# First chunk of an mLSTM and act-GCU kernel: the weight conversions in another order of steps, w_out's second piece ahead of the turning, the clamp on GpSimd

## The chip, the cores and the metric

The kernel runs on 1 core of a Trainium2 chip. The metric is the device time of one execution in microseconds (us). Before the change the median of 3 runs is 540.6 us (539.52 to 541.74).

## The reference, cut to what matters

```python
# B, H, S, D = 4, 8, 768, 40; n_tokens, d_model, d_ff = 3072, 320, 2048
def _attn_ref(q, k, v, i_gate, f_gate, o_gate):       # mLSTM cell, one step per t
    m_new = maximum(f[t] + m, i[t])
    C = exp(f[t] + m - m_new) * C + exp(i[t] - m_new) * outer(v[t], k[t])
    n = exp(f[t] + m - m_new) * n + exp(i[t] - m_new) * k[t]
    y[t] = sigmoid(o[t]) * (C @ q[t]) / maximum(abs(n . q[t]), 1.0)
    ...
def _moe_ref(x, w_in, w_out):                         # x: y as (3072, 320)
    h = x @ w_in                                      # 320 x 2048
    g = h * np.cos(h)
    return (g @ w_out).astype(np.float32)             # 2048 x 320

out["moe_" + k] = m[k]                                # float64
```

`w_in` and `w_out` (`np.random.randn` times a scale) reach the chip as float64, as pairs of 32-bit words. The kernel makes float32 of them itself. That conversion is what the change is about.

## The kernel before, in words

The sequence of 768 is cut into 6 chunks of 128 (`NC = 6`). One cell `n = c * B + b` is the mLSTM of chunk `c` and batch entry `b`, 8 heads at a time. `first_cells` does the cells of chunk 0. Then `both_parts(c, b)` runs for every chunk and every `b` of 0 to 3. It does cell `n = (c + 1) * B + b` of the next chunk beside a quarter of the second part for chunk `c`: `g = h * cos(h)` for 512 columns of `w_in`. It has two halves, `i = 0` and `i = 1`, each for 256 columns, `f2 = 2 * b + i`. I call `both_parts(0, b)` step b.

The order of the instructions on each engine is the order of the code (`tc.manual_schedule()`). Engines meet through semaphores, and a waiting instruction holds all behind it on its engine.

In a half, TensorE makes `h` for the 256 columns in two PSUM tiles `pup` (lines 639 and 645; two tiles in all, so the next half begins when the gates of this one are done). ScalarE rounds it (`near`, L653), VectorE takes the rest (`rest`, L656), ScalarE takes the sine (L661), VectorE multiplies (`gate`, L665). TensorE's product with `w_out` for the half before (`down`, L677) fills in between. Half 0 also has the cell's scores (L479), the weighting by them (`weigh`, L485), the values (L505 to L514), the normalising (L523 to L534, whose last product makes `xT`) and GpSimd's `fade` (L580). Half 1 has the cell's state (L622) and prepares the next cell: `turn_blocks` turns q and k with two VectorE transposes (L452), GpSimd scales q (`scale_q`, L461) and k (`weigh_k`, L407), and in step 1 ScalarE also copies low dimensions (L444).

The conversion. A piece is 128 rows by 512 elements of `w_in` (two for each step, p0 and p1), 128 by 256 of its last rows (`w_in_l`, the low piece), or 128 by 640 of `w_out`. It goes through five operations:

- ScalarE, `take_apart`: the absolute value of the high word taken as a float (L150), then the low word scaled (L152)
- VectorE, `put_together`: the clamp (L157), the two shifts in one instruction (L159), the sign put in with an `or` (L161, which reads the raw words too)
- GpSimd, `put_together`: the add of the low word's part (L162)

Raw words land in buffers that rotate: `pb`, 4 buffers, for `w_in`, and `pc`, 3 buffers, for `w_out`. The load of a piece into a buffer waits until the add (L162) of the piece that had it before is done. `w_out` has 8 pieces, o0 to o7: `next_out` converts the next one and issues the load of the piece 3 later. All these loads are issued by SyncE's queue (SP), one after the other, L180 for `w_out`, L139 (p0, then p1, four DMAs each) and L174 (low, four DMAs) for `w_in`.

Step b uses `w_in`'s pieces that were converted in the step before: step b's code converts p0, p1 and low for step b + 1, loads those for step b + 2 (`weights_in(b + 2)`, L1046), and converts `w_out` pieces o(2b) in half 0 and o(2b+1) in half 1. Where each conversion stands before the change:

- half 0, after the gates: p0 (L993, in steps 1 and 2), then `w_out` (L995)
- half 0, after the normalising: p0 in step 0, p1 in steps 1 and 2 (L1039)
- half 1, between `rest` and the state: p1 in step 0, low in steps 1 and 2 (L1002)
- half 1, after the gates: low in step 0 (L1013)
- half 1, at the end, after `weights_in` and after `turn_blocks` and `scale_q`: `w_out` (L1053)

In `first_cells` three pieces are converted, two of them with ScalarE's part done early.

Of the kernel before, what the change touches and what calls it, by code (L numbers as in the profile page):

```python
# [11 lines left out]
FP = mybir.dt.float32  # L12
I32 = mybir.dt.int32
# [3 lines left out]
OP = mybir.AluOpType  # L17
# [12 lines left out]
def kernel(  # L30
# [20 lines left out]
    nc = tc.nc  # L51
# [87 lines left out]
            nc.sync.dma_start(out=bits[rows, 0:n], in_=piece)  # L139
        return bits  # L140

    def to_float32(dst, bits):
        take_apart(dst, bits)
        put_together(dst, bits)

    def take_apart(dst, bits):
        n = dst.shape[1]
# [3 lines left out]

        nc.scalar.activation(out=bits[:, 0:n, 0], in_=lo, func=AF.Copy, scale=2.0 ** -29)  # L152

    def put_together(dst, bits):
        n = dst.shape[1]
        hi, t, m = bits[:, 0:n, 1], dst.bitcast(I32), bits[:, 0:n, 0]
        nc.vector.tensor_scalar(out=t.bitcast(FP), in0=t.bitcast(FP), scalar1=LEAST, scalar2=GREATEST,  # L157
                                op0=OP.max, op1=OP.min)
        nc.vector.tensor_scalar(out=t, in0=t, scalar1=5, scalar2=2, op0=OP.logical_shift_left,  # L159
                                op1=OP.logical_shift_right)  # L160
        nc.vector.scalar_tensor_tensor(out=t, in0=hi, scalar=TOP2, in1=t, op0=OP.bitwise_and, op1=OP.bitwise_or)  # L161
        nc.gpsimd.tensor_tensor(out=t, in0=t, in1=m, op=OP.add)  # L162

# [665 lines left out]
    def first_cells():  # L829
        nc.vector.memset(nil, 0.0)  # L830
        gates_in()
        nc.scalar.copy(out=ident_b, in_=ident)
        load(0, "qk")
        later_gates_in()
        load(0, "v")
        load(1, "qk")
        load_o(0, (0, 1))
        load(1, "v")
        load(2, "qk")
        load_E(0)  # L840
        load_E(1)
        warm(12)
        wall_in(0, 0, pmu)
        wall_in(0, 1, psum_o())
        gates_first()
        gates_first_out()
        spread(0, 0)
        decay_exponents_half(0, 0)
        turn(0)
        turn_out(0, False)  # L850
        gates_sums()
        spread(0, 1)
        decay_exponents_half(0, 1)
        decay(0)
        weigh_k(0)
        load_E(2)
        load(2, "v")
        load_E(3)
        load_o(0, (2, 3))
        load(3)  # L860
        pieces.extend(weights_in(0))
        wall_in(1, 0, psum_o())
        wall_in(1, 1, psum_o())
        gates_less_sums()
        spread(1, 0)
        decay_exponents_half(1, 0)
        scores(0)
        gates_maxima()
        turn(1)
        weigh(0)  # L870
        sigmoid(0, slice(0, 2))
        turn_out(1, False)
        spread(1, 1)
        decay_exponents_half(1, 1)
        gates_exponents()
        decay(1)
        weigh_k(1)
        values(0)
        normalize(0)
        scores(1)  # L880
        gates_exp()
        turn(2)
        turn_out(2, False)
        warm(2)
        seam(0)
        weigh(1)
        seam_out(0)
        state(0)
        load_two(B, "qk")
        decay_exponents(2)  # L890
        gates_diagonal()
        decay(2)
        weigh_k(2)
        values(1)
        load_E(B)
        normalize(1)
        scores(2)
        turn(3)
        sigmoid(0, slice(2, 4))
        seam(1)  # L900
        load_two(B, "Kv")
        load_E(B + 1)
        load_o(1)
        outs.append((0, weights_out(0)))
        weigh(2)
        decay_exponents(3)
        turn_out(3)
        seam_out(1)
        values(2)
        decay(3)  # L910
        weigh_k(3)
        state(1)
        normalize(2)
        scores(3)
        pg = gates_turn()
        warm(1)
        seam(2)
        weigh(3)
        to_float32(*pieces.pop(0))
        decay_exponents(B)  # L920
        pieces.extend(weights_in(1))
        outs.extend((p, weights_out(p)) for p in range(1, 3))
        seam_out(2)
        state(2)
        for piece in pieces[0:2]:
            take_apart(*piece)
        gates_keep(*pg)
        values(3)
        normalize(3)
        put_together(*pieces.pop(0))  # L930
        warm(3)
        seam(3)
        seam_out(3)
        put_together(*pieces.pop(0))
        low_dimensions(B)
        turn_blocks(B)
        state(3)
        load_E(B + 2)
        decay(B)
        sigmoid(1)  # L940
        weigh_k(B)
        odd_values(B)
        scale_q(B)
# [5 lines left out]

        nc.scalar.activation(out=spot, in_=spot, func=AF.Sin)  # L950

    def next_out():
        p, piece = outs.pop(0)
        to_float32(*piece)
        if p + 3 < NF // 2:
            outs.append((p + 3, weights_out(p + 3)))

    def both_parts(c, b):

        n = (c + 1) * B + b  # L960
        cell = n < N
        for i in range(2):
            f2 = 2 * b + i
            up = Up(c, f2)
            if cell and i == 0:
                scores(n)
                if c == 0 and b == 0:

                    warm(8, psum_o())
            if cell and i == 1:  # L970
                if n % 2 == 1 and n > B + 1 and n + 3 < N:
                    load_two(n + 3, "Kv")
            for e in range(2):
                up.near(e)
            for e in range(2):
                up.rest(e)
            if i == 0:
                if cell:
                    weigh(n)
                    if n + 1 < N:  # L980
                        decay_exponents(n + 1)
                    if n == B:
                        clear_low()
                for e in range(2):
                    up.sin(e)
                    up.gate(e)
                if c > 0:
                    sums(c, f2)
                if b == 0 and c == 1:
                    sigmoid(c + 1)  # L990

                if c == 0 and b > 0 and pieces:
                    to_float32(*pieces.pop(0))  # L993
                if c == 0:
                    next_out()  # L995
                if cell and n + 1 < N:
                    decay(n + 1)
            else:
                if cell:
                    seam_out(n)  # L1000
                if pieces:
                    to_float32(*pieces.pop(0))  # L1002
                if cell:
                    state(n)
                for e in range(2):
                    up.sin(e)
                    up.gate(e)
                if c > 0:
                    sums(c, f2)
                if n == B + 1:  # L1010
                    low_dimensions(n + 1)
                while pieces:
                    to_float32(*pieces.pop(0))  # L1013
                if cell and n + 1 < N:
                    weigh_k(n + 1)
                    odd_values(n + 1)
            if i == 1 and b == B - 1 and 0 < c < NC - 2:
                sigmoid(c + 2)
                sin_next()
            down_slot(c, f2)  # L1020
            if f2 == 0 and c > 1:
                for p in range(2):
                    combine_first(c - 1, p)
            if cell and i == 0:
                turn_gate(n)
                values(n)
                seam(n)
                normalize_turned(n)
                fade(n)
                if c == 1 and b < 3:  # L1030
                    weight_sums(b + 1)
                if n % 2 == 1 and n > B + 1 and n + 3 < N:
                    load_two(n + 3, "qk")
                if n > B + 1 and n + 3 < N:
                    load_E(n + 3)
                if b == B - 2 and c + 2 < NC:
                    load_o(c + 2)
                if c == 0 and pieces:
                    to_float32(*pieces.pop(0))  # L1039
                sin_next()  # L1040
            if f2 == 0 and c > 1:
                for p in range(2):
                    combine(c - 1, p)
            if i == 1:
                if c == 0 and b + 2 < B:
                    pieces.extend(weights_in(b + 2))  # L1046
                    load_two((n + 3) // 2 * 2)
                    load_E(n + 3)
                if cell and n + 1 < N:
                    turn_blocks(n + 1)  # L1050
                    scale_q(n + 1)
                if c == 0:
                    next_out()  # L1053
                if (c, f2) == (0, LAST):
                    weight_sums(0)

    pieces, outs = [], []
# [41 lines left out]
```

## Time and profile before

| | us |
|---|---|
| median of 3 runs | 540.6 (539.52 to 541.74) |
| the profiled execution | 540.66 |
| its span | 538.9 |
| TensorE (PE) busy in the span | 520.1 |
| VectorE (DVE) | 421.9 |
| ScalarE (ACT) | 285.7 |
| GpSimd (POOL) | 224.7 |
| mean granted TensorE clock | 0.972 |

The busy times are of the whole span. The change touches about 37 to 146 us of it, so the tables by stretch and the timeline of that stretch say more than the sums. In the timeline each row has its start, its length, its engine and line, what it writes and reads, and in brackets the idle time ahead of it and what ended it.

### The profile page before, as it was taken

What the parts mean: (1) busy time and instruction counts of PE and PEld (TensorE: products, weight loads), DVE (VectorE), ACT (ScalarE), POOL (GpSimd) and SP (SyncE); (2) the same over time, 40 slices, a digit from 0 to 9 for tenths busy, and PEclk for the clock granted to TensorE, in tenths of its full rate; (3) what the DMA queues carried; (4) which work ended last, traced back from release to release, by engine and by line L of the source; (5) the groups of instructions that cost most, each with busy time, mean ns of one, the idle gap of its engine ahead of it and who ended that gap; (6) DMA issues with size and microseconds to landing.
All of it is one profiled execution on the core that took longest, in us unless ns stands there. A gap on an engine that the chain in (4) does not pass through costs nothing.

```text
span 538.9 us, 10497 instructions
## 1 busy us (share of the span) xinstructions
PE 520.1 (97%) x3844; PEld 353.7 (66%) x3844; DVE 421.9 (78%) x907; ACT 285.7 (53%) x546; POOL 224.7 (42%) x369
## 2 busy tenths in 40 slices
PE   7999879899999999999999999999999999999996
PEld 4885445545566767757767767767667767576755
DVE  5565889998788897898878898878898878663636
ACT  2587958666475446826527826526836522222221
POOL 7435454555477573533542632542421421221211
PEclk9587989999999999999999999999999999999999
DMA  9999884959847539329248329249220000000001
GB/s 137 220 213 233 248 169 142 213 92 253 176 116 171 67 94 191 42 93 202 28 120 174 43 88 193 35 125 174 40 79 7 2 5 6 19 33 1 0 1 49
DMA packets 99939, 57.81 MB, mean 107 GB/s; under 512 B 62304, under 2 KB 92608, under 8 KB 99888
## 3 DMA queue, kind: packets, MB, share of 16 engines
q1 hardware_dynamic: 96496, 55.64, 47.4%
q10 hardware_dynamic: 3248, 1.33, 1.2%
q8 instruction: 30, 0.49, 0.4%
q0 software_dynamic: 144, 0.18, 0.1%
q14 instruction: 21, 0.17, 0.1%
HBM read 51.71 MB, written 4.11 MB: 104 GB/s over the span
## 4 chain that ended last, share of the span: by engine, by line
PE 73%; DMA 9%; DVE 8%; SPq 4%; POOL 2%; ACT 1%; issue 1%; DVEq 0%; POOLq 0%
PE pup L645 26%; PE acc L755 24%; PE pup L639 8%; PE po L677 3%; PE late L755 3%; DMA bits<-in_moe_w_in_dram 3%; PE ps L479 3%; PE vt L514 2%; PE vt L505 2%; PE pu L597 1%; DMA E<-M_d 1%; DVE t L452 1%; DMA xL<-xT 1%; DMA bits<-in_moe_w_out_dram 1%; DMA G<-G_d 1%
## 5 line engine op out<-in xcount | busy, mean ns | idle before, releaser
L645 PE MATMUL pup<-xT,w_in_sb 128*128 128x512 f32 x384 | 177.8, 606 | 4.8 <-DVE g L665 4.5
L653 ACT ACTIVATE n<-pup 128x512 int32<-128x512 f32 x96 | 54.0, 595 | 195.3 <-PE pup L639 143.7
L645 PEld LDWEIGHTS pup<-xT,w_in_sb 128*128 128x128 f32 x384 | 70.6, 193 | 92.2 <-issue 87.9
L656 DVE SCALAR_TENSOR_TENSOR n<-pup,n 128x512 f32<-128x512 f32 x96 | 63.1, 687 | 76.3 <-ACT n L653 75.0
L719 POOL TENSOR_TENSOR D<-g 128x128 f32<-128x128 f32 x40 | 19.8, 495 | 218.6 <-DVE g L665 218.6
L661 ACT ACTIVATE n<-n 128x512 f32<-128x512 f32 x96 | 57.6, 627 | 21.8 <-DVE n L656 13.1
L665 DVE SCALAR_TENSOR_TENSOR g<-pup,n 128x512 f32<-128x512 f32 x96 | 61.7, 684 | 4.1 <-ACT n L661 3.5
L755 PE MATMUL acc<-w_out_sb,g 128*128 128x160 f32 x320 | 58.6, 304 | 0.0
L755 PE MATMUL acc<-T,g 128*128 128x160 f32 x320 | 58.0, 301 | 0.1
L639 PE MATMUL pup<-xL,w_in_l 64*128 64x512 f32 x192 | 54.2, 641 | 0.0
L755 PEld LDWEIGHTS acc<-w_out_sb,g 128*128 128x128 f32 x320 | 47.8, 190 | 5.6 <-issue 4.2
L755 PEld LDWEIGHTS acc<-T,g 128*128 128x128 f32 x320 | 48.1, 190 | 3.6 <-issue 2.9
L402 ACT ACTIVATE E<-E,tab 128x128 f32<-128x128 f32 x160 | 49.0, 388 | 0.3
L677 PE MATMUL po<-w_out_sb,g 128*128 128x320 f32 x128 | 36.2, 436 | 1.8 <-POOL w_out_sb L162 1.8
L755 PE MATMUL acc<-T,S 128*128 128x160 f32 x160 | 35.0, 301 | 0.0
L479 PEld LDWEIGHTS ps<-t,t 40*128 40x128 f32 x384 | 26.0, 196 | 11.3 <-issue 6.6
L677 PEld LDWEIGHTS po<-w_out_sb,g 128*128 128x128 f32 x128 | 24.1, 190 | 13.2 <-POOL w_out_sb L162 2.4
L485 DVE TENSOR_TENSOR E<-ps,E 128x512 f32<-128x512 f32 x48 | 30.7, 681 | 0.5 <-PE ps L479 0.5
L461 POOL TENSOR_TENSOR qG<-t,G 128x512 f32<-128x512 f32 x20 | 25.6, 1281 | 13.0 <-DVE t L452 6.5
L639 PEld LDWEIGHTS pup<-xL,w_in_l 64*128 64x128 f32 x192 | 14.5, 185 | 23.3 <-issue 19.0
L755 PE MATMUL acc<-w_out_sb,S 128*128 128x160 f32 x160 | 28.8, 299 | 0.0
L950 ACT ACT_TABLE_LOAD x22 | 28.2, 1283 | 0.4
(175 smaller groups left out, 883.5 us busy)
## 6 DMA issues: line engine op xcount, KB each, us to landing
E<-M_d SPq DMA_DIRECT2D x22, 512.0 KB
qr<-in_q_dram SPq DMA_DIRECT2D x36, 160.0 KB
kr<-in_k_dram SPq DMA_DIRECT2D x36, 160.0 KB
G<-G_d SPq DMA_DIRECT2D x20, 256.0 KB
bits<-in_moe_w_out_dram SPq DMA_DIRECT2D x8, 640.0 KB
bits<-in_moe_w_in_dram SPq DMA_DIRECT2D x32, 128.0 KB
out_dram<-o_sb SPq DMA_DIRECT2D x24, 160.0 KB
ks<-in_k_dram SPq DMA_DIRECT2D x10, 320.0 KB
```

Source lines behind the costliest of these rows:

```text
L402: nc.scalar.activation(out=Es[n][:, h], in_=Es[n][:, h], func=AF.Exp, scale=-1.0, bias=tab[:, c, 0, g:g + 1])
L479: nc.tensor.matmul(ps[j][:, p], kT[r, p], qT[r, p], start=True, stop=True)
L485: nc.vector.tensor_tensor(out=w, in0=pss[n][j], in1=w, op=OP.mult)
L639: nc.tensor.matmul(pu, w_in_l[r, f2], xL[c][r].rearrange("p b t -> p (b t)"), start=ahead, stop=not ahead)
L645: nc.tensor.matmul(pu.rearrange("p (b t) -> p b t", b=B), w_in_sb[:, i, ts(2 * f2 + e, 128)], xT[c][:, i:NK * B:NK], start=(i == 0 and not ...
L653: nc.scalar.activation(out=self.n[e], in_=self.pu[e], func=AF.Copy, bias=0.25)
L656: nc.vector.scalar_tensor_tensor(out=self.n[e].bitcast(FP), in0=self.pu[e], scalar=0.25, in1=self.n[e], op0=OP.add, op1=OP.subtract)
L661: nc.scalar.activation(out=r, in_=r, func=AF.Sin, scale=TWO_PI_DOWN)
L665: nc.vector.scalar_tensor_tensor(out=g, in0=self.pu[e], scalar=TWO_PI, in1=self.n[e].bitcast(FP), op0=OP.mult, op1=OP.mult)
L677: nc.tensor.matmul(po[c][b], gs[c, f][:, ts(b, C)], w_out_sb[:, f], start=(f == 0), stop=(f == NF - 1))
L755: nc.tensor.matmul(a, lhs, rhs, start=start, stop=stop)
L950: nc.scalar.activation(out=spot, in_=spot, func=AF.Sin)
```

## The change

The conversion becomes four loops over any number of pieces: first ScalarE's part of all, then the clamp of all on GpSimd, then the shifts of all, then `or` and add of all. Two pieces of `first_cells` keep the clamp on VectorE. In half 0 of steps 1 and 2 p0 and `w_out` go through it together. In half 1 the conversion between `rest` and the state goes away: all pieces that are left and `w_out` go through together after the gates, ahead of `weights_in`, `turn_blocks` and `scale_q`. In chunk 0 `weigh_k` moves behind `scale_q`.

```diff
-    def to_float32(dst, bits):
-        take_apart(dst, bits)
-        put_together(dst, bits)
+    def to_float32(*made):
+        for dst, bits in made:
+            take_apart(dst, bits)
+        for dst, bits in made:
+            bound(nc.gpsimd, dst)
+        for dst, bits in made:
+            shift_out(dst)
+        for dst, bits in made:
+            put_together(dst, bits)
...
+    def bound(engine, dst):
+        engine.tensor_scalar(out=dst, in0=dst, scalar1=LEAST, scalar2=GREATEST, op0=OP.max, op1=OP.min)
+
+    def shift_out(dst):
+        t = dst.bitcast(I32)
+        nc.vector.tensor_scalar(out=t, in0=t, scalar1=5, scalar2=2, op0=OP.logical_shift_left,
+                                op1=OP.logical_shift_right)
+
     def put_together(dst, bits):
         n = dst.shape[1]
         hi, t, m = bits[:, 0:n, 1], dst.bitcast(I32), bits[:, 0:n, 0]
-        nc.vector.tensor_scalar(out=t.bitcast(FP), in0=t.bitcast(FP), scalar1=LEAST, scalar2=GREATEST,
-                                op0=OP.max, op1=OP.min)
-        nc.vector.tensor_scalar(out=t, in0=t, scalar1=5, scalar2=2, op0=OP.logical_shift_left,
-                                op1=OP.logical_shift_right)
         nc.vector.scalar_tensor_tensor(out=t, in0=hi, scalar=TOP2, in1=t, op0=OP.bitwise_and, op1=OP.bitwise_or)
         nc.gpsimd.tensor_tensor(out=t, in0=t, in1=m, op=OP.add)
...
+        bound(nc.vector, pieces[0][0])
+        shift_out(pieces[0][0])
         put_together(*pieces.pop(0))
...
-    def next_out():
+    def next_out(*made):
         p, piece = outs.pop(0)
-        to_float32(*piece)
+        to_float32(*made, piece)
         if p + 3 < NF // 2:
             outs.append((p + 3, weights_out(p + 3)))
...
-                if c == 0 and b > 0 and pieces:
-                    to_float32(*pieces.pop(0))
                 if c == 0:
-                    next_out()
+                    next_out(*[pieces.pop(0) for _ in range(min(b, len(pieces), 1))])
...
-                if pieces:
-                    to_float32(*pieces.pop(0))
                 if cell:
                     state(n)
...
-                while pieces:
-                    to_float32(*pieces.pop(0))
+                if c == 0:
+                    next_out(*pieces)
+                    pieces.clear()
                 if cell and n + 1 < N:
-                    weigh_k(n + 1)
+                    if c > 0:
+                        weigh_k(n + 1)
                     odd_values(n + 1)
...
                 if cell and n + 1 < N:
                     turn_blocks(n + 1)
                     scale_q(n + 1)
-                if c == 0:
-                    next_out()
+                    if c == 0:
+                        weigh_k(n + 1)
```

On the engines this is 18 clamps fewer on VectorE and 18 more on GpSimd (7 of 512 elements, 3 of 256, 8 of 640). On SP the load of o4 stands ahead of `weights_in(2)` and that of o6 ahead of `weights_in(3)`, where they stood behind them and behind the loads of q, k, v and E that follow.

More of the change, by code (lines that the diff above doesn't have):

```diff
@@ L918, in first_cells @@
         weigh(3)
-        to_float32(*pieces.pop(0))
+        to_float32(pieces.pop(0))
         decay_exponents(B)
@@ L933, in first_cells @@
         seam_out(3)
+        bound(nc.vector, pieces[0][0])
+        shift_out(pieces[0][0])
         put_together(*pieces.pop(0))
@@ L1011, in both_parts @@
                     low_dimensions(n + 1)
-                while pieces:
-                    to_float32(*pieces.pop(0))
+                if c == 0:
+                    next_out(*pieces)
+                    pieces.clear()
                 if cell and n + 1 < N:
-                    weigh_k(n + 1)
+                    if c > 0:
+                        weigh_k(n + 1)
                     odd_values(n + 1)
@@ L1038, in both_parts @@
                 if c == 0 and pieces:
-                    to_float32(*pieces.pop(0))
+                    to_float32(pieces.pop(0))
                 sin_next()
```

## The prediction, before the run

> **What bounds the kernel now.** I read the windows first, cut at the four steps of chunk 0 (busy us of PE, PEld, DVE, ACT, POOL; granted clock, DMA share, GB/s):
>
> ```profile
> 57.40:80.30 22.90, 20.03 (x129) 10.91 (x120) 21.00 (x45) 16.19 (x32) 11.29 (x12) 0.93 0.81 201
> 80.30:103.30 23.00, 21.11 (x145) 12.29 (x144) 21.59 (x45) 17.41 (x35) 11.43 (x13) 1.00 0.69 178
> 103.30:126.30 23.00, 21.38 (x146) 12.48 (x145) 21.57 (x45) 15.08 (x29) 11.19 (x12) 1.00 0.72 149
> 126.30:148.00 21.70, 21.70 (x148) 12.97 (x148) 16.89 (x36) 13.21 (x24) 9.81 (x12) 1.00 0.88 199
> ```
>
> VectorE works 21.0 to 21.6 of 23 us in steps 0 to 2. In step 3, without w_in, TensorE never stops and a step takes 21.7. So 124.68, where step 3's first `down` starts, is the last place where conversions decide. Next TensorE's rows in the timeline, where its idle time stands:
>
> ```profile
> 70.71 5.37 PE L645 MATMUL pup<-xT,w_in_sb 128*128 128x512 f32 x8 [2.41 <-DVE g L665]
> 95.40 3.67 PE L645 MATMUL pup<-xT,w_in_sb 128*128 128x512 f32 x8 [1.19 <-DVE g L665]
> 118.37 3.67 PE L645 MATMUL pup<-xT,w_in_sb 128*128 128x512 f32 x8 [0.94 <-DVE g L665]
> 124.68 4.58 PE L677 MATMUL po<-w_out_sb,g 128*128 128x320 f32 x16 [0.68 <-POOL w_out_sb L162]
> ```
>
> At each step's end it waits for the gate of half 1. The same eight matmuls take 5.37 us after the long wait, since the clock is at 0.50 from 72.5 to 75.5. The idle time of steps 0 to 2 is 6.4 us (2.9, 1.9 and 1.6: stretch less PE busy), 1.7 more are that clock (5.37 for 3.67): 8 us is the most that can be won. Then SP's queue, and VectorE beside GpSimd:
>
> ```profile
> 62.28 0.38 SPq L180 DMA_DIRECT2D bits<-in_moe_w_out_dram  x1
> 62.71 8.50 SPq L139 DMA_DIRECT2D bits<-in_moe_w_in_dram  x8
> ```
> ```profile
> 192.06 0.86 POOL L701 TENSOR_TENSOR T<-w_out_sb 128x320 f32<-128x320 f32 x1
> 193.00 0.86 POOL L702 TENSOR_TENSOR w_out_sb<-w_out_sb 128x320 f32<-128x320 f32 x1
> ```
> ```profile
> 83.50 1.48 DVE L159 TENSOR_SCALAR w_out_sb<-w_out_sb 128x640 int32<-128x640 int32 x1
> 193.27 1.01 DVE L534 TENSOR_TENSOR xT<-yt,db 128x384 f32<-128x384 f32 x1
> ```
>
> Piece p0 for step 2 is issued at 62.71 and read by ScalarE at 79.72: far ahead. The last two rows are VectorE instructions held by GpSimd: the shift takes 0.49 alone and 1.48 beside the add of p0 (83.20 to 84.63); `xT` takes 0.56 alone and 1.01 beside L702, which ends at 193.86.
>
> **Prices** (start to next start, us, for 512 / 640 / 256 elements): shift 0.46 / 0.53 / 0.33, `or` 0.61 / 0.74 / 0.34, add 1.25 / 1.54 / 0.69; ScalarE's pair 1.14 / 1.49 / 0.69; two rests 1.20, state 0.9, two gates 1.2, two transposes 1.87, `fade` 1.35. The clamp on GpSimd is in no row. Nearest is affine_select, also one input with a compare per element: 1.091 for 1024 and 0.292 for 128 elements, a line that gives 0.63 / 0.75 / 0.41. Low bound, the memsets (0.204 for 128, 1.186 for 1312): 0.52 for 512. High bound, the add: 1.30 / 1.57 / 0.74. I take the first: same shape of work. The GPSIMD Engine Reference of the Trainium skill (3.1, Elementwise) gives about one cycle per element for loops of few operations, an estimate of 0.43 plus dispatch for 512; by it the sum below would be about 1 us smaller, and no run so far shows it.
>
> **What goes.** 18 clamps leave VectorE: 7 x 0.42 + 3 x 0.28 + 8 x 0.49 = 7.7 us, and the three shifts held to 1.44 to 1.48 are freed of 3 x 0.97 = 2.9. GpSimd gets 7 x 0.63 + 3 x 0.41 + 8 x 0.75 = 11.6; it has 11 us of work in 23, so there is room, but the clamps now stand between ScalarE and VectorE, in order. `weigh_k` behind `scale_q` costs nothing: its reader, `pu`, starts over 5 us later. In `first_cells` the clamp (0.63) ends when `weigh` does: nothing.
>
> **What comes, step by step.**
>
> Step 0, half 1. The rests stay at 66.25 (ScalarE's table load sets them). Without p1 ahead of the state the gates end at 69.7, before 71.2: 1.5 won. Now three pieces go together. ScalarE ends the sine at 68.2, then p1 and low; w_out's absolute value ends at 70.8, its clamp at 71.6, so VectorE, its other shifts done, stands until then: shift 72.2, `or` of p1 72.8, low 73.2, w_out 75.25, because add and `or` alternate as L534 and L702 do. Adds: p1 74.5, low 76.0, w_out 77.5. Before, p1 was there at 70.5: step 1's `h` starts its second 128 rows 4 us later, but then has no further gap, and `down` needs the add of 77.5 (before 78.45). About even.
>
> SP. The load of o4 waits for that add, and `weights_in(2)` now stands behind it: 77.5 for 62.7. Two such loads, w_out then p0, take 4.4 us: issued from 62.28, the windows show 112, 275, 234 and 38 GB/s from 62.0 in pieces of 1.5 us, done by 66.7. So p0 lands at L = 81.9; ScalarE wants it at 79.7. Behind p0 in ScalarE's queue stand w_out, the exponentials, p1 and `near`; the twelve loads and those of q and k behind them end before 90, ahead of their readers (93).
>
> Step 1, half 0, from L: p0's value +0.65, clamp +1.36; w_out's value +1.93, clamp +2.78, shift +3.4, both `or` +4.7; the normalising 3.9 more (oT 85.76 to the clamp at 89.68), 0.2 held by `fade`: +8.9. Adds end +7.6, `fade` +8.95, p1's clamp +9.6 (behind `fade`), shift and `or`, +0.2 for the two holding each other: rest at L + 10.9 = 92.8, before 91.21. Half 1: rests, state, gates 3.3: 96.1, before 95.85 (low is no longer in between). Then ScalarE: sine to 94.7, low dimensions 1.7, low 0.7, w_out's value 97.8, clamp 98.6, shift 99.2, `or`s 100.3, transposes 102.2; add of o3 at 102.65. Step 2's rest starts at 102.9, before 100.85.
>
> Step 2, the same with o6 ahead of `weights_in(3)`: L = 102.65 + 4.4 = 107.05 (issued at 92.34 before); rest 118.0 (114.18), gates 121.3 (118.75), ScalarE's w_out value 121.4, clamp 122.2, `or`s 123.9, transposes 125.8, scores 126.8, then step 3's `down`: 126.8, before 124.68. From here TensorE has no gap in either kernel.
>
> Sum: +2.1. Span 538.9 + 2.1 = 541.0; the profiled run is 540.66 and the median 540.6, so 542.7.
>
> SBUF — State Buffer of the Trainium skill (Who interferes with whom) speaks against this change: an instruction of VectorE with two inputs in SBUF and one of GpSimd that reads SBUF exclude each other for their whole length. The trace agrees (1.01 for 0.56). `or` reads two.
>
> **Rivals.**
> - The relief comes through. If the adds come early enough that p0 lands by 79.7 (add of o1 by 75.3), VectorE has 0.42 + 0.49 + 0.97 less behind half 0's gates and 0.42 + 0.55 less before half 1's, TensorE finds the gates done at 93.7 when its `down` ends, and `h`, w_out's shift, `or` and the transposes put step 2's rest at 99.2 (before 100.85); the same again in step 2: -3.3, 537.3. For it: VectorE's own work allows an add at 74.3 to 75.4. Against it: ScalarE's w_out value at 70.8.
> - `or` and add do not hold each other. The three-piece batch ends 1.0 earlier, and three of the four batches behind it, those that lead on to the end, 0.75 each: -3.3 on the sum, 539.4. Against it: L534.
> - Slower: GpSimd's clamp runs at the add's price. In each half 0 w_out's clamp is 0.9 and p1's 0.65 later, in each half 1 w_out's 0.8: 0.8 + 2 x 2.35 = 5.5 more, 548.2. It decides from about 0.75 for 512 elements.
> - The clock. TensorE idles 70.9 to 74.5 in step 0, and up to 1.9 us in steps 1 and 2 (for w_in_l and the gate). Before, 2.4 us of idling were followed by 3.3 us at 0.50, 1.7 us lost. Once or twice more on the path: 544.4 to 546.1. For it: the gap is longer. Against it: step 1's path runs through SP's queue, not TensorE.
>
> **How the numbers follow.** About 0.5% (2.7 us) is what a measurement of this kernel can tell. Forecast 0.38, relief 0.24, no hold 0.14, clamp 0.14, clock 0.10. Predicted 542.7. The forecast's own range is 541 to 544.5 (landing 4 to 5 us after issue, clamp 0.52 to 0.75). The others widen it: 537.0 to 547.5. Faster than 537.9: most of the relief case, 0.22. Slower than 543.3: clamp, clock, and a third of the forecast, 0.38. Within: 0.40.
>
> **What would show it.** SP: L139's second group issued near 77, not 62.7, right after the add of o1; the third near 103. ScalarE idle at L150 in steps 1 and 2, ended by a DMA of w_in. The clamp's mean for 512 near 0.63. Shifts of w_out at 0.49. VectorE busy about 2.5 us less a step, with waits for the clamp in their place. Wrong if ScalarE never waits for w_in, if the clamp is over 1 us, or if step 3's `down` starts before 124.

## The result, and the profile after

| | before | after |
|---|---|---|
| time, median (lowest to highest) | 541.04 us (539.52 to 541.74) | 560.45 us (559.99 to 560.72) |
| ratio, 95% interval | | 1.0368 (1.0339 to 1.0397) |
| profiled run, its span | 540.66, 538.9 us | 559.99, 558.2 us |
| VectorE / GpSimd busy | 421.9 / 224.7 us | 416.2 / 262.2 us |

The change made the kernel 3.7% slower; 0.4% was predicted. The stretches are cut this time where the first `h` of each step starts (columns: stretch; busy us of PE, PEld, VectorE, ScalarE, GpSimd; granted clock, DMA share, GB/s), for the changed kernel:

```profile
43.03:68.43 25.40, 21.00 (x139) 10.85 (x137) 17.25 (x37) 21.87 (x46) 16.64 (x17) 0.92 0.85 230
68.43:103.00 34.57, 24.26 (x145) 13.09 (x145) 21.43 (x41) 16.58 (x33) 24.71 (x19) 0.90 0.59 131
103.00:136.11 33.11, 25.19 (x145) 14.21 (x145) 18.88 (x39) 17.30 (x34) 22.64 (x19) 0.90 0.60 122
136.11:159.15 23.04, 21.43 (x145) 12.48 (x145) 16.97 (x35) 13.76 (x25) 14.86 (x14) 1.00 0.58 149
```

and for the kernel before, with the same cuts:

```profile
46.76:70.71 23.95, 19.51 (x138) 10.52 (x137) 19.01 (x41) 23.67 (x50) 13.03 (x15) 0.97 0.80 228
70.71:95.40 24.69, 23.03 (x145) 12.99 (x145) 22.99 (x47) 16.58 (x33) 12.94 (x14) 0.93 0.72 168
95.40:118.37 22.97, 21.33 (x144) 12.43 (x145) 21.56 (x44) 16.54 (x31) 11.44 (x14) 1.00 0.65 128
118.37:140.22 21.85, 21.17 (x144) 12.60 (x145) 18.09 (x36) 12.78 (x23) 8.58 (x11) 1.00 0.88 221
```

Steps 1 and 2 are 9.9 and 10.1 us longer, steps 0 and 3 1.5 and 1.2. That is 22.7 us (116.12 for 93.46); the span grew by 19.3, because `first_cells` ran 3.7 us faster in this execution. From 15 to 27 us the kernel before had a granted clock of 0.50, the changed one 0.72. The profiles of the experiments start their first `h` at 42.3 to 42.7 or at 46.7 to 46.9 us; kernels in the changed order show both, the three profiles in the old order only the later, and whether the change has a part in it stays open.

In steps 1 and 2 VectorE has less work than before, and GpSimd has twice the work. The groups of GpSimd's clamp in the changed kernel (count; busy us, mean ns of one; idle time before):

```profile
L161 POOL TENSOR_SCALAR w_out_sb<-w_out_sb 128x640 f32<-128x640 f32 x8 | 18.7, 2342 | 8.9 <-ACT w_out_sb L156 5.6 <-DVE g L675 3.2
L161 POOL TENSOR_SCALAR w_in_sb<-w_in_sb 128x512 f32<-128x512 f32 x7 | 13.4, 1918 | 12.1 <-ACT w_in_sb L156 11.8
...
L161 POOL TENSOR_SCALAR w_in_l<-w_in_l 128x256 f32<-128x256 f32 x3 | 3.2, 1061 | 3.5 <-ACT w_in_l L156 3.5
```

One clamp of 512 elements lasts 1.92 us, three times the 0.63 of the prediction and above its upper end of 1.30. Who waits for it stands in the table of waits from 56 to 165 us (total, times, longest):

```profile
DVE w_in_sb L165 <- POOL w_in_sb L161: 15.6, 6, 6.1
...
DVE w_out_sb L165 <- POOL w_out_sb L161: 13.4, 8, 2.4
...
PEld po L687 <- POOL w_out_sb L172: 7.4, 3, 3.9
PE pup L655 <- DVE g L675: 7.2, 3, 3.0
...
PE pup L655 <- POOL w_in_sb L172: 5.6, 1, 5.6
```

VectorE stands 29 us for the clamps of w_in and w_out, and TensorE for what comes behind: the gates, the adds of w_out, and once, at the start of step 1, the add of p1 out of step 0's batch of three pieces. SP's queue, which the prediction followed, and ScalarE's first operation on p0 behind it:

```profile
61.11 18.04 SPq L190 DMA_DIRECT2D bits<-in_moe_w_out_dram  x2
79.20 4.52 SPq L139 DMA_DIRECT2D bits<-in_moe_w_in_dram  x8
...
95.36 16.39 SPq L190 DMA_DIRECT2D bits<-in_moe_w_out_dram  x2
111.80 4.97 SPq L139 DMA_DIRECT2D bits<-in_moe_w_in_dram  x8
```
```profile
85.82 0.67 ACT L156 ACTIVATE w_in_sb<-bits 128x512 f32<-128x512 f32 x1 [1.64 <-DMA bits<-in_moe_w_in_dram]
118.80 0.70 ACT L156 ACTIVATE w_in_sb<-bits 128x512 f32<-128x512 f32 x1 [5.12 <-DMA bits<-in_moe_w_in_dram]
```

w_in for step 2 is issued at 79.20 in place of 62.71, for step 3 at 111.80 in place of 92.34, each time right behind the load of w_out that waits for an add. ScalarE then waits 1.6 and 5.1 us for it. So both suspects are in the trace, one of them larger than thought. TensorE's own lines show what follows:

```profile
103.00 3.67 PE L655 MATMUL pup<-xT,w_in_sb 128*128 128x512 f32 x8 [3.03 <-DVE g L675]
109.88 1.13 PE L649 MATMUL pup<-xL,w_in_l 64*128 64x512 f32 x4 [3.22 <-POOL w_in_l L172]
...
112.75 5.79 PE L687 MATMUL po<-w_out_sb,g 128*128 128x320 f32 x16
...
128.39 6.27 PE L687 MATMUL po<-w_out_sb,g 128*128 128x320 f32 x16 [3.03 <-POOL w_out_sb L172]
136.11 3.67 PE L655 MATMUL pup<-xT,w_in_sb 128*128 128x512 f32 x8 [1.45 <-DVE g L675]
143.60 4.57 PE L687 MATMUL po<-w_out_sb,g 128*128 128x320 f32 x16
```

Behind the longer idle times the same sixteen matmuls take 5.79 and 6.27 us for 4.57: 2.9 us more. The granted clock is 0.79 and 0.73 in these two stretches, 1.00 from 143.60 on. Step 3's first `down` starts at 143.60; it was 124.68.

### The profile page after: what moved, and what is told of

Read it like the earlier page. It is cut to its first block, busy times and chain, and to the rows that moved or that the text cites. A ratio compares the mean times of both kernels' runs of the same rounds, so it can differ in the third digit from the quotient of the medians.

```text
span 558.2 us, 10495 instructions
## 1 busy us (share of the span) xinstructions
PE 522.1 (94%) x3844; PEld 350.7 (63%) x3844; DVE 416.2 (75%) x889; ACT 285.5 (51%) x546; POOL 262.2 (47%) x387
## 3 DMA queue, kind: packets, MB, share of 16 engines
q1 hardware_dynamic: 96496, 55.64, 46.9%
## 4 chain that ended last, share of the span: by engine, by line
PE 73%; DMA 10%; DVE 7%; SPq 3%; POOL 2%; issue 2%; ACT 2%; ACTq 0%; DVEq 0%; POOLq 0%
PE pup L655 25%; PE acc L765 23%; PE pup L649 7%; PE ps L489 4%; DMA G<-G_d 3%; DMA bits<-in_moe_w_in_dram 3%; PE late L765 3%; PE vt L524 2%; PE vt L515 2%; PE po L687 2%; PE pu L607 1%; DMA xL<-xT 1%; SPq L184 1%; PE pw L837 1%; DVE t L462 1%
## 5 line engine op out<-in xcount | busy, mean ns | idle before, releaser
L687 PE MATMUL po<-w_out_sb,g 128*128 128x320 f32 x128 | 39.4, 464 | 4.9 <-POOL w_out_sb L172 4.9
L687 PEld LDWEIGHTS po<-w_out_sb,g 128*128 128x128 f32 x128 | 25.4, 203 | 18.6 <-POOL w_out_sb L172 7.4
L489 PE MATMUL ps<-t,t 40*128 40x128 f32 x384 | 27.8, 286 | 1.3 <-DVE t L462 1.3
```

The source lines that it names most:

```text
L489: nc.tensor.matmul(ps[j][:, p], kT[r, p], qT[r, p], start=True, stop=True)
L687: nc.tensor.matmul(po[c][b], gs[c, f][:, ts(b, C)], w_out_sb[:, f], start=(f == 0), stop=(f == NF - 1))
```

## The experiments

Theory L: the length of GpSimd's clamp, in series between ScalarE and VectorE, costs most. Theory Q: SP's order does, loads of w_in behind a load of w_out that waits for an add. All ratios are to the kernel before.

**1. The clamp back on VectorE** (everything else as changed).

```diff
-            bound(nc.gpsimd, dst)
+            bound(nc.vector, dst)
```


> The changed kernel with its clamps back on VectorE; the order of steps, the groups and SP's order stay as changed. Theory L (length): the clamp's 1.92 us for 512 and 2.34 us for 640 elements on GpSimd, in series between ScalarE and VectorE in each batch, is what costs. Then a batch is shorter by some 1.4 to 1.9 us for each clamp on its path, the add that SP's queue waits for comes 3 to 5 us earlier, and most of the 19.4 us returns: 541 to 546. Theory Q (queue): loads of w_in standing behind the load of w_out on SP are what costs, whatever the clamp's engine. Then only what the clamps themselves last is won, and the third group of w_in loads is still issued near 108 to 111: 551 to 556.

Measured: 544.6 us, 1.012 (1.0069 to 1.0171). About 2.5% of the 3.7 went with the clamp. What is left is more than nothing: ScalarE still waits 2.5 and 4.6 us for w_in.

**2. The load of w_out late.** `next_out` of half 1 converts, and its load is issued at the step's end, behind those of w_in, q, k and E (`late=True` leaves the load out of `next_out`).

```diff
-                    next_out(*pieces)
+                    p = next_out(*pieces, late=True)
...
+                if c == 0 and p < NF // 2:
+                    outs.append((p, weights_out(p)))
                 if (c, f2) == (0, LAST):
```


> The changed kernel with the load of w_out's piece in half 1 issued at the end of the step, behind the loads of w_in, q, k and E; the clamps stay on GpSimd. Theory L: ScalarE no longer waits for w_in, which was 1.6 us in step 1 and 5.1 us in step 2, and nothing else is won, since the clamps stay in series: 553 to 557. Theory Q: the steps are as long as before the change: 541 to 546.

Measured: 553.88 us, 1.0298 (1.0251 to 1.0346): 0.7% won, and no wait of ScalarE for w_in is left. While the clamp is long the queue is the lesser limit.

**3. Both edits.**

> Both edits: clamps on VectorE and the load of w_out behind those of w_in; the changed order of steps and groups is all that is left of the change. Theory L: a little under the run with the clamps on VectorE alone, by the 0 to 3 us that SP's hold still cost there: 538 to 543. Theory Q: about the run with the late load alone, 538 to 544. If the grouping itself costs (VectorE's or-instructions and GpSimd's adds holding each other, 0.8 us a batch): 543 to 546.

Measured: 537.32 us, 0.9976 (0.9943 to 1.0008). Nothing is left of the loss. Against the first run the queue is worth 1.4% here, for 0.7% in the second run. That each of the two hides behind the other would explain it, but the intervals of the four ratios are too wide to show it. The grouping of steps, the rest of the change, costs nothing that can be measured.

**4. The old order with the clamp on GpSimd alone.**

```diff
-        put_together(dst, bits)
+        put_together(dst, bits, nc.gpsimd)
...
-    def put_together(dst, bits):
+    def put_together(dst, bits, engine=nc.vector):
...
-        nc.vector.tensor_scalar(out=t.bitcast(FP), in0=t.bitcast(FP), scalar1=LEAST, scalar2=GREATEST,
+        engine.tensor_scalar(out=t.bitcast(FP), in0=t.bitcast(FP), scalar1=LEAST, scalar2=GREATEST,
```


> The kernel before, with only the clamps of the same 18 pieces moved to GpSimd; order, single pieces and SP's order as before. Theory L: each clamp of 512 elements is 1.9 us in place of 0.42 between ScalarE and VectorE, now piece by piece without another piece's work beside it; the batch before the state in half 1 has two in a row: 555 to 570. Theory Q: SP's order is that of before, so little is lost: 541 to 546.

Measured: 557.83 us, 1.0376 (1.0324 to 1.0429). The clamp alone, in the old order and the old queue, loses as much as the whole change.

**5. The old kernel with the loads of w_in, q, k and E behind the load of w_out.**

```diff
-                if c == 0 and b + 2 < B:
-                    pieces.extend(weights_in(b + 2))
-                    load_two((n + 3) // 2 * 2)
-                    load_E(n + 3)
...
                 if c == 0:
                     next_out()
+                if c == 0 and b + 2 < B:
+                    pieces.extend(weights_in(b + 2))
+                    load_two((n + 3) // 2 * 2)
+                    load_E(n + 3)
```


> The kernel before, with nothing changed but the place of the loads of w_in, q, k and E: at the step's end behind the load of w_out, which waits for an add of GpSimd. Theory Q2 (the queue's hold is a cost of its own, about 7 us, as between the last two runs with the clamp on VectorE): the second group of w_in loads goes out near 78.5 and the third near 103 to 106, 11 us and more later than before, ScalarE waits 2 to 6 us for w_in twice: 544 to 549. Theory S (slack: the hold only hurts together with the grouped order, in which three pieces share a batch): under 1% more, 539 to 542.

Measured: 550.55 us, 1.0184 (1.0146 to 1.0223). Two lines of SP's queue and the table of ScalarE's waits in this kernel:

```profile
79.22 4.59 SPq L139 DMA_DIRECT2D bits<-in_moe_w_in_dram  x8
...
107.28 4.42 SPq L139 DMA_DIRECT2D bits<-in_moe_w_in_dram  x8
```
```profile
ACT w_in_sb L150 <- DMA bits<-in_moe_w_in_dram: 12.8, 2, 7.0
```

The hold is a cost of its own, in the old order too: ScalarE waits 5.8 and 7.0 us, where 2 to 6 us each were expected, and the time lies above the 544 to 549 of theory Q2, so the hold costs more than that theory said.

**6. One operation in place of two** (a look at prices; one run, 561.07 us).

```diff
-            bound(nc.gpsimd, dst)
+            if dst.shape[1] == WP:
+                nc.gpsimd.tensor_scalar(out=dst, in0=dst, scalar1=LEAST, scalar2=None, op0=OP.max)
+            elif dst.shape[1] > WP:
+                nc.gpsimd.tensor_scalar(out=dst, in0=dst, scalar1=1.0, scalar2=None, op0=OP.mult)
+                bound(nc.vector, dst)
+            else:
+                bound(nc.gpsimd, dst)
```


> A look at prices, not at the time: the changed kernel where GpSimd does only the max on pieces of 512 elements (the min is left out), one multiplication by 1.0 on pieces of 640 (their clamp is done by VectorE) and both operations of the clamp on pieces of 256. If each operation of the instruction is a pass over the data: 0.95 to 1.0 us for 512 and 1.2 for 640, 1.06 still for 256. If the form costs 3.7 ns an element whatever it does: 1.92, 2.34 and 1.06.

Measured, in the groups of GpSimd (the third line is affine_select, the row that the prediction took its price from):

```profile
L149 POOL TENSOR_SCALAR w_out_sb<-w_out_sb 128x640 f32<-128x640 f32 x8 | 14.5, 1816 | 12.7 <-ACT w_out_sb L162 12.5
...
L147 POOL TENSOR_SCALAR w_in_sb<-w_in_sb 128x512 f32<-128x512 f32 x7 | 10.5, 1493 | 11.8 <-ACT w_in_sb L162 11.5
L404 POOL TENSOR_SCALAR_AFFINE_SELECT E<-E 128x1024 f32<-128x1024 f32 x7 | 7.7, 1100 | 4.3 <-DMA bits<-in_moe_w_in_dram 3.0 <-DMA E<-M_d 1.2
```

Neither expectation holds. One operation takes 1.49 us for 512 and 1.82 for 640: 2.5 ns an element and 0.2 us, if the max on 512 and the multiplication on 640 cost the same. Two take 3.3 ns and 0.22 us. So the second operation adds 0.8 ns an element; the first, with all else that the instruction does for an element, costs 2.5, near the add of two tensors (1.25 us for 512), and nothing like affine_select (0.9 ns by the prediction's line). Why the two differ so is not settled.

**7. The early p1.** On top of the third run, step 0's half 0 takes one piece of w_in as the other steps do, since the third run's trace showed what still cost: TensorE waits 3.12 us for the add of p1 out of the batch of three, and step 1 takes 26.1 us at a clock of 0.93.

```diff
-                    next_out(*[pieces.pop(0) for _ in range(min(b, len(pieces), 1))])
+                    next_out(*[pieces.pop(0) for _ in range(min(len(pieces), 1))])
```


> The kernel with clamps on VectorE and late load of w_out, and in step 0 one piece of w_in in half 0's batch, as in steps 1 and 2, so that the batch of half 1 has two pieces and not three. Theory: the changed order gains in steps 2 and 3 (22.4 and 21.0 us a step for 23.0 and 21.9 before) and gives it back at the start of step 1, where TensorE waits 3.1 us for GpSimd's add of p1 and then runs at a lower clock (26.1 us). Without that wait: 533 to 536, 0.5 to 1% under the kernel before. Rival: half 0's gates of step 0 or its state come later by the piece put there, and the time stays: 536.5 to 539.

Measured: 534.05 us, 0.9894 (0.9863 to 0.9924). Steps 1 to 3, third run and this kernel's second profile:

```profile
69.25:95.38 26.13, 23.01 (x144) 12.97 (x145) 22.34 (x47) 17.20 (x34) 13.85 (x13) 0.93 0.66 150
95.38:117.76 22.38, 21.36 (x145) 12.43 (x144) 20.21 (x45) 17.58 (x34) 12.68 (x13) 1.00 0.68 149
117.76:138.79 21.03, 21.03 (x146) 12.53 (x145) 16.58 (x37) 12.94 (x24) 8.84 (x10) 1.00 0.95 222
```
```profile
68.36:89.74 21.38, 21.36 (x144) 12.48 (x145) 19.89 (x44) 16.30 (x32) 12.45 (x12) 1.00 0.77 170
89.74:111.97 22.23, 21.36 (x145) 12.41 (x144) 20.24 (x45) 17.42 (x33) 12.69 (x13) 1.00 0.70 162
111.97:133.00 21.03, 21.03 (x146) 12.50 (x145) 16.80 (x38) 12.81 (x24) 8.84 (x10) 1.00 0.94 223
```

Step 1 falls from 26.1 to 21.4 us, and TensorE idles less than 1 us in the three steps together. So the changed order can bring TensorE to steps without gaps, as the prediction's first rival hoped, but here with the clamps on VectorE; the batch of three in step 0 gave it back.

**8. The clamp of w_out a batch ahead on GpSimd** (on top of the third run, ScalarE's operations moved ahead with it; the first of the eight pieces has no batch ahead of it, and VectorE clamps it, so GpSimd has seven).

```diff
...
+        if ahead:
+            take_apart(*ahead)
+            bound(nc.gpsimd, ahead[0])
...
```


> The kernel with clamps on VectorE and late load of w_out, except that the clamp of each w_out piece is done by GpSimd one batch ahead (ScalarE's two operations too), while VectorE works on the pieces of this batch: the same 2.34 us of GpSimd eight times, now without anybody behind it in line. Theory L (the length costs only where the clamp stands in series): no slower than with the clamps on VectorE, 534 to 538. Rival (a long GpSimd instruction costs wherever it stands, by holding VectorE's instructions or delaying the adds behind it): 540 to 546.

Measured: 557.03 us, 1.0321 (1.0281 to 1.0361): theory L missed by its number. But steps 1 and 2 took 26.3 and 22.5 us, as in the third run. In the profiled execution (553.10 us, the fastest of six) most of the loss is one wait, made by the edit, in the batch at the end of step 2, whose low piece TensorE then waits 10.5 us for:

```profile
129.52 0.77 ACT L167 ACTIVATE w_out_sb<-bits 128x640 f32<-128x640 f32 x1 [11.01 <-DMA bits<-in_moe_w_out_dram]
```

The piece read ahead was issued by SP at 121.85 only, behind loads that wait for buffers.

**9. A quarter of the clamp, the length that was predicted.** GpSimd clamps the first quarter of the columns; the clamp of the others is left out.

```diff
-            bound(nc.gpsimd, dst)
+            bound(nc.gpsimd, dst[:, 0:dst.shape[1] // 4])
```


> The changed kernel, but GpSimd clamps only the first quarter of each piece's columns (the clamp of the other three quarters is left out), so that the instruction should last what the prediction's first price was. From the lengths of both operations (1.92 us for 512, 1.06 for 256: 0.22 and 3.3 ns an element) 128, 160 and 64 columns take 0.64, 0.75 and 0.43 us, for 0.63, 0.75 and 0.41 predicted. Everything else of the change is there. If the price was the prediction's only wrong step: the predicted ratio, 1.004 (542.7 over 540.6), third group of w_in loads issued near 103. If the price was the greater of two wrong steps, and the landing of w_in behind w_out's load (4.4 us taken, 6.6 to 7.0 seen) the other: two landings at 2.2 to 2.6 us more each, 1.012 to 1.015. If the price was not the cause at all: 1.03 and more.

Measured: 546.49 us, 1.0131 (1.0091 to 1.0172), with clamps of 0.64, 0.75 and 0.44 us (0.63, 0.75 and 0.41 predicted). The predicted ratio, 1.004, lies below the interval: the price was the larger wrong step, and there was a second one. SP's queue and ScalarE in this kernel:

```profile
77.41 4.42 SPq L139 DMA_DIRECT2D bits<-in_moe_w_in_dram  x8
...
104.78 4.89 SPq L139 DMA_DIRECT2D bits<-in_moe_w_in_dram  x8
```
```profile
83.85 0.68 ACT L156 ACTIVATE w_in_sb<-bits 128x512 f32<-128x512 f32 x1 [2.43 <-DMA bits<-in_moe_w_in_dram]
111.78 0.67 ACT L156 ACTIVATE w_in_sb<-bits 128x512 f32<-128x512 f32 x1 [5.12 <-DMA bits<-in_moe_w_in_dram]
```

p0 lands 6.4 and 7.0 us after its issue.

**10. The early p1 again, 11. with the load of w_out directly behind those of w_in, 12. and with the clamp ahead on that.** The three shared one chip.

> The same kernel as the one with the early p1, again, as the measure for the next two on this chip: 0.986 to 0.993 of the kernel before.

> The kernel with the early p1, and the load of w_out directly behind those of w_in, ahead of those of q, k, v and E, which wait for buffers. Theory: in step 3 ScalarE's wait for w_out (2.8 us) goes; it is little or nothing on the path, since TensorE has no idle time there: within 0.3% of the kernel with the early p1. Rival: SP now waits at w_out for GpSimd's add ahead of the loads of q and k, and these come late for the turning: 0.5% and more slower.

> The same, with the clamp of each w_out piece a batch ahead on GpSimd. The look at the first trial of it showed steps 1 and 2 as long as with the clamp on VectorE (26.3 and 22.5 us for 26.1 and 22.4), and one wait of 11.0 us of ScalarE for a load of w_out that SP issued only at 121.85; that load is now issued before the clamp needs it. Theory L (length costs only in series): within 0.5% of the run just before. Rival (a long GpSimd instruction costs wherever it stands): 1% and more slower.

Measured: 534.06 us, 0.9915 (0.9888 to 0.9942); 534.11 us, 0.9911 (0.9881 to 0.9942); 538.23 us, 0.9972 (0.9945 to 1.0). The place of the load makes no difference. The last one is 0.6% slower than the run before it, between what the two theories said. Its steps 1 to 3 take 64.9 us from the first `h` (73.02 to 137.88), for 64.6 with the early p1 (68.36 to 133.00): the five clamps that GpSimd does in them (2.34 to 2.49 us each), off the series, cost nothing that shows. Step 0 is longer, from half 1's `h` to the next step 13.9 us for 10.7 (lines of its table of waits from 56 to 72 us):

```profile
PEld po L698 <- POOL w_out_sb L183: 4.9, 1, 4.9
...
ACT w_out_sb L167 <- DMA bits<-in_moe_w_out_dram: 2.8, 1, 2.8
```

Its first batch reads a second piece of w_out before it has landed, and GpSimd's clamp of that piece stands ahead of the adds that `down` waits for. So theory L holds for a clamp that nobody stands behind. A place for all of them was not found, and no run with clamps on GpSimd was faster than the one with the early p1 and the clamps on VectorE.

## Why the prediction was wrong

Point by point, with the ninth run as the kernel in which the clamp has the predicted price (its first `h` starts at 46.79, before's at 46.76, so the times can be set beside each other; after started 3.7 us earlier):

| | predicted | quarter clamp | after |
|---|---|---|---|
| step 1's first `h` (gates of step 0) | 69.7 | 69.74 | 68.43 |
| w_in for step 2 issued | 77.5 | 77.41 | 79.20 |
| p0 landed | 81.9 | 83.85 | 85.82 |
| step 2's first `h` (gates of step 1) | 96.1 | 97.60 | 103.00 |
| w_in for step 3 issued | 102.65 | 104.78 | 111.80 |
| p0 landed | 107.05 | 111.78 | 118.80 |
| step 3's first `h` (gates of step 2) | 121.3 | 125.52 | 136.11 |
| step 3's first `down` | 126.8 | 131.47 | 143.60 |

**The step that failed first: the price of the clamp.** "Nearest is affine_select, also one input with a compare per element": it was not near. The clamp took 1.92, 2.34 and 1.06 us for 0.63, 0.75 and 0.41. The high bound, the add (1.30), was no bound either: one operation of the clamp's form alone took 1.49 in the sixth run. The estimate of 0.43 plus dispatch that stood beside the price lay further off still. From the ratios with the quarter and with the whole clamp, 1.0131 and 1.0368, the price was worth 2.4%, some 13 us of the 17.8 by which the time lay above the prediction. The mechanism was that of the rival "GpSimd's clamp runs at the add's price"; the rival's rule (two clamps in each half 0, one in each half 1, all in series) fits, its price was too small: by the table, steps 1 and 2 are 6.7 and 5.2 us longer with the whole clamp than with the quarter, and the rival had 2.35 for each. A cheap clamp on GpSimd was as good as one on VectorE (1.0131 and 1.012).

**The second: the landing.** "Two such loads, w_out then p0, take 4.4 us" was read from SP's row of 8.50 us with x8. The row begins with the first issue, and the other seven were not there. Cut at 67.0 us, the same queue of the kernel before shows one, cut at 69.0 four; and its table of waits has the gap of 4.9 us (the transfer named there is the one that came last by the profile, so what held the second issue stays open):

```profile
62.71 0.47 SPq L139 DMA_DIRECT2D bits<-in_moe_w_in_dram  x1
```
```profile
62.71 6.65 SPq L139 DMA_DIRECT2D bits<-in_moe_w_in_dram  x4
```
```profile
SPq L139 <- DMA xL<-xT: 4.9, 1, 4.9
```

So of the two loads 640 + 128 KB moved in those 4.4 us, not 640 + 4 x 128. The prediction's own windows had the sign: 1.5 us each at 112, 275, 234 and 38 GB/s are 0.99 MB, less than the 1152 KB of both loads. An estimate scaled by the bytes, 4.4 x 1152 / 768, gives 6.6 us; the quarter clamp shows 6.4 and 7.0, after 6.6 and 7.0. The excess over 4.4 in the quarter clamp, 2.0 and 2.6 us, is nearly all of the 4.7 us by which step 3's first `down` came later than predicted (131.47 for 126.8); between the ratios 1.004 and 1.0131 lie 4.9 us. What came behind a landing was right: half 1's first `rest` starts 10.83 us after it in both steps of the quarter clamp (94.68 and 122.61), for 10.9 predicted.

**Right:** step 0's gates; the hold of SP and its times, as long as the clamp's price was that of the prediction (77.41 for 77.5); ScalarE's waits at p0 in steps 1 and 2; the shifts of w_out, which went back to 0.49; TensorE without a gap from step 3's first `down` on (15.55 us busy of 15.55 from 143.60 to 159.15 in after), so that all that is lost before it reaches the end. VectorE had 1.6 and 2.7 us less work in steps 1 and 2 (22.99 to 21.43, 21.56 to 18.88), near the 2.5 predicted in step 2 and less in step 1, and waits for the clamp in its place.

**`or` and add.** They hold each other, as the Trainium skill has it in SBUF — State Buffer (Who interferes with whom), and the rival that denied it fell. In the batch of three, after's timeline shows

```profile
74.72 1.90 DVE L171 SCALAR_TENSOR_TENSOR w_out_sb<-bits,w_out_sb 128x640 int32<-128x640 int32 x1
```

for 0.82 alone. But only there: in the batches of two it is the add that waits (1.75 for 1.29 in the quarter clamp, 1.80 in after), 0.5 us and not the 0.75 that the prediction took.

**The other rivals.** "The relief comes through" needed the adds early enough, and neither the clamp nor the queue let them be; with both undone, and without the batch of three, TensorE's gaps went (the seventh run), but the clamps were then on VectorE, so a VectorE relieved of them was never seen to win. The clock's rival happened too, as a follower: 2.9 us in the two `down` groups shown above, each behind a wait of TensorE.

## What to carry to other kernels

An operation that no row shows should be priced by a row with the same instruction form on the same engine, and where there is none, the range has to reach as far as the dearest elementwise row counted once for each operation (here two adds, 2.5 us for 512, with 1.92 measured); a single measurement of it settles more than the whole sum. A merged row of a queue (one start, one length, xN) hides when the N were issued: cut the window before taking a landing time from it. When a short operation is put on a slower engine between two others, count the hand-over once for every piece in series, and look which load's issue waits for the last of them.

## What had not been expected of the hardware

GpSimd's TENSOR_SCALAR costs 2.5 ns an element for one operation and 3.3 for two (1.49 and 1.92 us for 512), while VectorE does the same clamp in 0.42. And a clamp of 2.5 us on GpSimd (by its span, which the profiler gives only roughly) did not hold VectorE's two-input instructions for its whole length. The eighth run's timeline (first line GpSimd, then VectorE):

```profile
72.17 2.53 POOL L172 TENSOR_SCALAR w_out_sb<-w_out_sb 128x640 f32<-128x640 f32 x1 [3.88 <-ACT w_out_sb L167]
72.42 1.20 DVE L182 SCALAR_TENSOR_TENSOR w_in_sb<-bits,w_in_sb 128x512 int32<-128x512 int32 x1
73.55 0.41 DVE L182 SCALAR_TENSOR_TENSOR w_in_l<-bits,w_in_l 128x256 int32<-128x256 int32 x1
73.88 0.81 DVE L182 SCALAR_TENSOR_TENSOR w_out_sb<-bits,w_out_sb 128x640 int32<-128x640 int32 x1
```

The first `or` takes 1.20 us for 0.69; the other two run at their usual 0.41 and 0.81 while the clamp is still on. That differs from the Trainium skill, SBUF — State Buffer (Who interferes with whom), by which the two would exclude each other for a whole instruction; beside the add they do. At nine of the fourteen clamps of the eighth and the twelfth run one instruction of VectorE near the clamp's start, an `or` or a shift, is 0.4 to 0.5 us longer than usual, and those behind it are not.
